# Top-k attention, dense layer and routed experts in one kernel: every batch in two groups of rows, epsilon on VectorE, loads and routing reordered

## The chip, the core and the metric

One core of a Trainium2 chip runs the whole program. TensorE (PE) multiplies, with its weight loads shown as a row of their own (PEld), VectorE (DVE) and ScalarE (ACT) do element work, GpSimd (POOL) does element work and issues some transfers, SyncE (SP) issues the others. The metric is the device time of one execution in microseconds (us).

## The reference

Three layers follow each other.

```python
scores = (q @ k.T) / 8                      # 4 batches, 8 heads, 576 rows, head size 64
mask = scores >= kth_largest(scores, 32)    # per row of 576
attn = exp(where(mask, scores, -1e9) - max)
x = attn / (attn.sum() + 1e-9) @ v          # -> 2304 tokens x 512
h = x @ w_in                                # 512 -> 2048
x = (max(h, 0) + alpha * min(h, 0)) @ w_out # 2048 -> 512
go = x @ w_skip > 0                         # which tokens take an expert
e = argmax(x @ w_gate)                      # which of 8 experts
out = x + go * gate[e] * relu(x @ w1[e]) @ w2[e]   # 512 -> 1024 -> 512
```

All products are computed in parts: each float32 operand is split into a high and a low part, and three matmuls (high by high, low by high, high by low) stand for one.

## The kernel before, in words

**Units.** The attention of one batch has four pairs of heads. A pair has five units: units 0 to 3 hold 128 rows of each of the two heads, unit 4 (the mixed one) the last 64 rows of both. `Unit` has one method per piece of work: `scores` (PE), `copy` (ACT), `fold` and four `round`s (DVE, they find the 32nd largest), `exp` (ACT), `weights` (DVE, mask and sum, L449), `eps` (ACT, L454, adds 1e-9 to the sum), `recip` (DVE, L458, and ACT's broadcast L461), `turn` (PE transposes), `evac` (ACT), `values` (PE), `out` (DVE, ACT, POOL).

**The order around it.** `main` walks over the units in steps. A step has 14 slots; the table `STEP` says in which slot which method runs, and for which unit relative to the step's own. Units are spread over about five steps: scores two steps ahead, values one step behind. In each slot `slot(q)` then issues pieces of the dense layer from the list `todo`, as many as the budget q allows. Over a step the budget is what is left divided by the steps that are left, at least BMIN = 4.3 and at most BMAX = 6.0 us by the kernel's own cost figures, and half of it in a step whose next unit is mixed. Six matmuls of n columns cost 6 n / 2400 us in this table. An engine does its instructions in the order in which they were issued.

**Groups.** `work` lists groups of rows: (batch, units, first column, column tiles). Batch 0 is two groups, units 0 and 1 (256 rows) and units 2 to 4 (320 rows). Batches 1 to 3 are one group each, with two column tiles of 288. For each group all four pairs are done, and each pair loads and turns q and k (`heads`: `load`, `turn` for q and k, `turn_t` for the last 64 rows). When a group's attention is complete, `queue_moe` puts its dense layer (`moe1`) on the list, so the dense layer of a batch is computed beside the attention of the next one; the dense layer of the last group has nothing left beside it.

**The dense layer.** `moe1` streams the weights in 16 chunks of 1 MB through three buffers (`wr`, issued by POOL, L525). A chunk serves all column tiles of the group: 48 matmuls of 288 columns for a group with two tiles, 24 matmuls for a group with one. With two tiles the hidden layer is done in two halves (`nhf = 2`), and the second half's result is added by POOL (L640); with one tile there is one pass.

**Rows and routing.** After a group's dense layer `rows` computes the routing scores (`logits`, PE), `route`, `rest` and `slots` (some 30 small DVE instructions) and writes the rows out. A hook, `pick`, runs after batch 2 and chooses the expert whose first block is prepared early.

**After the attention.** A loop calls `slot(TS)` until the lists are empty. It counts its turns (`gone`, from `pick` on): from the 39th turn it loads expert weights ahead (`wraw`, 0.5 MB each, issued by SP, L950), and splits them into high and low parts (ACT L956, DVE L957). Eleven blocks of 128 tokens follow: gather, first layer (L985), second layer (L1003), write.

**Buffers.** The input of the dense layer is a tile x per batch, two of them in turn. The first `out` of batch b waits until the dense layer of batch b - 2 is complete (`getx`), and issues what is left of it at once.

Of the kernel before, what the change touches and what calls it, by code (L numbers as in the profile page):

```python
# [35 lines left out]
AHEAD = 2  # L36
EC = 32
PH = 9
ECC = 1.9
CL = 2  # L40
# [9 lines left out]
HL = 3  # L50
# [9 lines left out]
def kernel(  # L60
# [240 lines left out]

    def heads(b, p, i):

        hd = dict(vb=vbd[i], qb=qbd[i])
        nats = {}

        def load():

            hd["q"] = att.tile([128, 2, SB], F32R, name="qT", tag="qT", bufs=2)
            hd["k"] = att.tile([128, 2, S + TL], F32R, name="kT", tag="kT", bufs=2)  # L310
# [16 lines left out]
        def turn(s):  # L327
            pt = ptile()
            for r in range(SF):
                nc.tensor.transpose(pt[:, r * 128:(r + 1) * 128], nats[s][:, r].rearrange("p h d -> p (h d)"), ident)  # L330
            c0 = TL
            late.append((HL, lambda: part(hd["k"][:, :, c0:c0 + SB] if s else hd["q"], pt)))

        def turn_t():
            pt = ptile()
            nc.tensor.transpose(pt[:, 0:128], nats[2].rearrange("p h d -> p (h d)"), ident)

            def copies():

                raw = att.tile([128, 512], F32, name="raw_", tag="raw_", bufs=2)[:, 0:TL]  # L340
# [5 lines left out]
                part(hd["k"][:, :, 0:TL], pt[:, TL:128])  # L346
                nc.gpsimd.tensor_copy(hd["k"][:, :, S:S + TL], hd["k"][:, :, 0:TL].bitcast(F32))

# [10 lines left out]
        hd["v"] = loadv  # L359
        return hd, [load, lambda: turn(0), lambda: turn(1), turn_t]  # L360

    class Unit:
# [317 lines left out]
    def rows(b, us, colof, x2t, hook, then):  # L680
# [394 lines left out]
    def main(work, exact, hooks=(lambda: [], lambda: [])):  # L1075

        if not exact:
# [4 lines left out]
            todo.insert(4, (0.5, late_consts))  # L1082
        steps, pairs, colofs, bases = [], [], [], []
        stream.clear()
# [4 lines left out]
        for wi, (b, us, col0, cols) in enumerate(work):  # L1089
# [5 lines left out]
            for p in range(NP):  # L1095
                pairs.append((b, p))
                for u in us:
                    steps.append((wi, len(pairs) - 1, u))
# [5 lines left out]
        hds, hq, vq = {}, [], {}  # L1104

        def push_heads(i):
            hd, parts = heads(*pairs[i], i % 2)
            hds[i] = hd
            hq.extend(parts)
            if i > 1:  # L1110

# [28 lines left out]
        def queue_moe(wi):  # L1140
# [11 lines left out]
            def then():  # L1152
                rowq.extend(rows(b, us, colofs[wi], x2t, hooks[1] if wi + 1 == len(work) else none[0],
                                 hooks[0] if wi + 2 == len(work) else none[0]))

# [29 lines left out]
        for kx in range(-2, K + 2):  # L1185
# [19 lines left out]
            for x in range(NSLOT):  # L1205
# [3 lines left out]
                for at, d, name, *a in STEP:  # L1209
                    if at != x:  # L1210
                        continue
                    if name == "heads":
                        for f in hmine:
                            f()
# [11 lines left out]

    T2 = [(0, 288), (288, 576)]
# [193 lines left out]
```

## Time and profile before

| | us |
|---|---|
| median of 3 runs | 1147.65 (1147.05 to 1148.07) |
| profiled execution, time | 1146.64 |
| its span, first to last instruction | 1144.8 |
| DVE busy in the span | 957.6 (84%) |
| PE busy | 976.2 (85%) |
| ACT busy | 738.7 (65%) |
| POOL busy | 453.9 (40%) |

The time is 1.84 us above the span. Shares over the whole span mix stages with different limits: attention (with the conversion of the dense layer's weights at its start), a stretch with the last dense layer alone, and the blocks of the experts. Busy time of PE is modelled and includes the depth of its pipeline. A line is a group of records of one source line; an idle time is put down to what ended it.

### The profile page before, as it was taken

Reading aid. Unit: us, or ns where it says so; the run is one execution under the profiler, and the core shown is the slowest. Engines: PE = TensorE matmul, PEld = TensorE weight load, DVE = VectorE, ACT = ScalarE, POOL = GpSimd, SP = SyncE. Lnnn points to the kernel's source line nnn. Section 1 sums busy time; section 2 is a strip of 40 time slices with the busy share of each in tenths; the row PEclk is TensorE's granted clock in tenths of the full one; section 3 lists DMA queues with packets and bytes.
Section 4 is the critical chain, followed back from the end, with each engine's and each line's share of the span. In section 5 each row is a group of like instructions: output and inputs, shape, how many; then the busy total and the mean of one; then the engine's idle time right before and its main releaser. Section 6 shows DMA issues by size and latency. Waiting matters only on the chain.

```text
span 1144.8 us, 21810 instructions
## 1 busy us (share of the span) xinstructions
PE 976.2 (85%) x7214; PEld 855.7 (75%) x7214; DVE 957.6 (84%) x2906; ACT 738.7 (65%) x1970; POOL 453.9 (40%) x591
## 2 busy tenths in 40 slices
PE   1255657989898987898998999899999999898996
PEld 1143436879777875787997998789899999687884
DVE  5799999999999999999999889999933331799872
ACT  5576666866777665776677567767734452597761
POOL 5445543643334331244235344423435343228111
PEclk9996566999999995899999999999999999799998
DMA  8977764567544530224324253332337863699870
GB/s 233 336 220 229 216 184 124 188 191 232 187 136 154 179 130 21 69 75 142 97 84 142 75 171 93 105 122 75 112 111 274 298 221 111 195 372 385 316 276 15
DMA packets 129771, 197.37 MB, mean 172 GB/s; under 512 B 62766, under 2 KB 92462, under 8 KB 119408
## 3 DMA queue, kind: packets, MB, share of 16 engines
q1 hardware_dynamic: 115632, 107.48, 29.9%
q0 software_dynamic: 14016, 88.40, 22.6%
q8 instruction: 59, 0.97, 0.3%
q14 instruction: 64, 0.52, 0.2%
HBM read 167.44 MB, written 29.71 MB: 172 GB/s over the span
## 4 chain that ended last, share of the span: by engine, by line
PE 42%; DVE 42%; ACT 5%; issue 4%; DMA 4%; POOL 2%; SPq 1%; POOLq 0%; DVEq 0%; ACTq 0%
PE pm L627 14%; DVE v L420 8%; PE pm L578 8%; DVE F L411 6%; DVE Ex L449 6%; DVE F L423 5%; DVE m L411 5%; PE px L1003 4%; PE pm L985 3%; PE px L510 3%; PE pt L476 3%; PE ps L390 3%; DVE rn L595 3%; DMA nat<-in_q_dram 2%; DVE cv L278 2%
## 5 line engine op out<-in xcount | busy, mean ns | idle before, releaser
L627 PE MATMUL pm<-g,wr 128*128 128x288 f32 (+2 forms) x1536 | 237.3, 303 | 7.2 <-POOL g L109 7.2
L578 PE MATMUL pm<-x,wr 128*128 128x288 f32 (+2 forms) x1536 | 238.9, 304 | 4.0 <-ACT x L519 2.9
L627 PEld LDWEIGHTS pm<-g,wr 128*128 128x128 f32 x1536 | 209.0, 189 | 15.1 <-POOL g L109 8.8
L578 PEld LDWEIGHTS pm<-x,wr 128*128 128x128 f32 x1536 | 211.2, 191 | 10.4 <-issue 5.3
L420 DVE MAX8 v<-F 128x8 f32<-128x72 f32 (+2 forms) x576 | 214.0, 406 | 1.0
L395 ACT ACTIVATE sb<-ps 128x288 f32<-128x288 f32 x288 | 104.9, 411 | 89.3 <-PE ps L390 70.3
L109 POOL TENSOR_TENSOR g<-rn,g 128x288 fp32r<-128x288 f32 (+2 forms) x128 | 108.2, 853 | 123.2 <-ACT g L609 52.5
L390 PE MATMUL ps<-kT,qT 64*128 64x288 f32 x768 | 106.4, 363 | 38.6 <-ACT sb L395 15.7
L449 DVE SCALAR_TENSOR_TENSOR Ex<-sb,v,Ex 128x576 f32<-128x576 f32 x144 | 124.5, 891 | 0.0
L423 DVE MATCH_REPLACE8 F<-v,F 128x72 f32<-128x72 f32 (+1 forms) x432 | 122.7, 289 | 0.0
L390 PEld LDWEIGHTS ps<-kT,qT 64*128 64x128 f32 x768 | 69.2, 210 | 68.2 <-ACT sb L395 19.8
L109 POOL TENSOR_TENSOR x<-xf,x 128x128 fp32r<-128x128 f32 (+1 forms) x80 | 38.7, 483 | 177.6 <-ACT x L519 164.6
L443 ACT ACTIVATE Ex<-sb,st 128x576 f32<-128x576 f32 x144 | 105.0, 780 | 0.0
L595 DVE SCALAR_TENSOR_TENSOR rn<-rn,nalpha 128x288 f32<-128x288 f32 (+2 forms) x128 | 72.5, 566 | 34.3 <-ACT rn L589 31.7
L476 PE MATMUL pt<-ident,Ex 128*128 128x128 f32 x576 | 92.6, 302 | 0.0
L510 PE MATMUL px<-PT,vt 128*64 128x128 f32 (+1 forms) x1280 | 92.0, 292 | 0.0
L488 ACT ACTIVATE PT<-pt 128x512 f32<-128x512 f32 x144 | 86.0, 598 | 2.3 <-PE pt L476 2.0
L588 ACT ACTIVATE rn<-pm 128x288 f32<-128x288 f32 (+2 forms) x128 | 52.7, 412 | 45.3 <-PE pm L578 44.6
L476 PEld LDWEIGHTS pt<-ident,Ex 128*128 128x128 f32 x576 | 72.2, 154 | 11.1 <-issue 6.5
L510 PEld LDWEIGHTS px<-PT,vt 128*64 128x64 f32 x1280 | 72.5, 150 | 10.2 <-issue 2.9
L411 DVE TENSOR_TENSOR F<-m 128x144 f32<-128x144 f32 (+2 forms) x240 | 78.2, 377 | 0.0
L609 ACT ACTIVATE g<-rn 128x288 fp32r<-128x288 f32 (+2 forms) x128 | 56.4, 448 | 23.0 <-DVE rn L595 22.9
(367 smaller groups left out, 1839.2 us busy)
## 6 DMA issues: line engine op xcount, KB each, us to landing
wraw<-in_moe_w_dram SPq DMA_DIRECT2D x88, 512.0 KB, 6.0
wr<-win POOLq DMA_DIRECT2D x40, 1024.0 KB, 5.2
wr<-wout POOLq DMA_DIRECT2D x40, 1024.0 KB, 5.2
cv<-in_moe_w_in_dram SPq DMA_DIRECT2D x16, 512.0 KB, 5.3
win<-cv SPq DMA_DIRECT2D x16, 512.0 KB, 5.4
cv<-in_moe_w_out_dram SPq DMA_DIRECT2D x16, 512.0 KB, 4.1
wout<-cv SPq DMA_DIRECT2D x32, 256.0 KB, 4.5
vt<-in_v_dram SPq DMA_DIRECT2D x20, 256.0 KB, 3.0
```

Source lines behind the costliest of these rows:

```text
L109: i = nc.gpsimd.tensor_tensor(o, a, b, op=OP.subtract)
L390: nc.tensor.matmul(self.ps[h, j][:, 0:HALF], lhsT=hd["q"][gp, a, u * 128:(u + 1) * 128], rhs=hd["k"][gp, b_, c0:c0 + HALF], **se)
L411: gate[0] = nc.vector.tensor_tensor(o[:, n_], a[:, n_, 0:w], a[:, n_, w:2 * w], op=op)
L420: nc.vector.max(v8[:, h, r, :], F[:, h, 0:w])
L423: nc.vector.match_replace(out=F[:, h, 0:w], in_to_replace=v8[:, h, r, :], in_values=F[:, h, 0:w], imm_value=NEG)
L443: nc.scalar.activation(self.Ex[:, h, :], self.sb[:, h, :], AF.Exp, bias=self.st[:, 0, h:h + 1], scale=0.125)
L449: nc.vector.scalar_tensor_tensor(Ex[:, h, :], sb[:, h, :], v8[:, h, 3, 7:8], Ex[:, h, :], op0=OP.is_ge, op1=OP.mult, accum_out=st[:, 1, h: ...
L476: nc.tensor.transpose(pt[:, c * 128:(c + 1) * 128], P[:, c0:c0 + 128], ident)
L510: nc.tensor.matmul(x[h * 64:(h + 1) * 64, 0:n], lhsT=hd["vt"][:, h, c, :], rhs=rhs, start=False, stop=(c == SF - 1))
L578: nc.tensor.matmul(hp[:, 0:n], lhsT=w[:, (f % 2) * 8 + a * 4 + d, :], rhs=x[:, d, c0:c1], start=(i == 0), stop=(i == 3 * KD - 1))
L595: nc.vector.scalar_tensor_tensor(rn[:, 0, 0:n], rn[:, 1, 0:n], nalpha[:, f:f + 1], rn[:, 0, 0:n], op0=OP.mult, op1=OP.add)
L627: nc.tensor.matmul(op_[:, 0:n], lhsT=w[:, 2 * f + a, :], rhs=g[(hf + ch) * 8 + f, sg][:, gg, 0:n], start=(i == 0), stop=(i == ni - 1))
```

## The change

- `work` gives every batch as two groups, units 0 and 1 (one tile of 256 columns) and units 2 to 4 (one tile of 320). There are eight groups and 32 pairs for five groups and 20 pairs.
- `heads` loads and turns only the q rows of its own group; k is loaded and turned whole for each group, and q's last 64 rows only where unit 4 is in it. The loads of a pair are put on SP's list one pair earlier, and the turns are split over two slots of a step.
- `eps` (ACT) goes; `recip` does the addition on DVE, and moves from slot 5 to slot 2, ahead of round 0. ACT's broadcast stays in slot 5 as `spread`.
- `route` follows `logits` three slots later, for one (RD).
- `pick` is tied to the last group of batch 2.

```diff
+RD = 3
+WHOLE = ()
-        (1, 2, "copy", 0), (1, -1, "eps"),
-        (2, 1, "round", 0),
+        (1, 2, "copy", 0),
+        (2, -1, "recip"), (2, 1, "round", 0),
...
-        (5, -1, "recip"), (5, -1, "turn", 1),
+        (5, -1, "spread"), (5, -1, "turn", 1),
...
-        (10, 0, "heads"), (10, 0, "weights", 0), (10, -1, "evac", 2),
+        (10, 0, "heads", 0), (10, 0, "weights", 0), (10, -1, "evac", 2),
         (11, 0, "weights", 1),
+        (12, 0, "heads", 1),
...
-    def heads(b, p, i):
+    def heads(b, p, i, us):
...
+        full = [u for u in us if u < SF]
+        own = ((full[0], full[-1] + 1), (0, SF))
...
+                r0, r1 = own[s]
                 for h in range(2):
-                    nc.sync.dma_start(nat[:, :, h, :], src[b, 2 * p + h, 0:SB, :].rearrange("(p r) d -> p r d", p=128))
+                    nc.sync.dma_start(nat[:, r0:r1, h, :],
+                                      src[b, 2 * p + h, 0:SB, :].rearrange("(p r) d -> p r d", p=128)[:, r0:r1])
...
-        def eps(self):
-            st = self.st
-            nc.scalar.activation(st[:, 1, self.n_], st[:, 1, self.n_], AF.Copy, bias=1e-9)
-
         def recip(self):
             st = self.st
+            nc.vector.tensor_scalar(st[:, 1, self.n_], st[:, 1, self.n_], 1e-9, None, op0=OP.add)
             nc.vector.reciprocal(st[:, 2, self.n_], st[:, 1, self.n_])
+
+        def spread(self):
+            st = self.st
...
-        parts = [(lambda: not early[0] and rroom(), None), (0.1, logits), (0, None), (0.1, route)]
+        parts = [(lambda: not early[0] and rroom(), None), (0.1, logits)] + [(0, None)] * RD + [(0.1, route)]
...
-    work = [(0, [0, 1], 0, [(0, 256)]), (0, [2, 3, 4], 256, [(256, 576)])]
-    for b in range(1, B - 1):
-        work.append((b, [0, 1, 2, 3, 4], 0, T2))
-    work.append((B - 1, [0, 1, 2, 3, 4], 0, T2))
+    work = []
+    for b in range(B):
+        if b in WHOLE:
+            work.append((b, [0, 1, 2, 3, 4], 0, [(0, 288), (288, 576)]))
+        else:
+            work += [(b, [0, 1], 0, [(0, 256)]), (b, [2, 3, 4], 256, [(256, 576)])]
```

Three places show what moves. On DVE, in a step of the attention, before (L458 is the reciprocal, 420 and 423 the rounds, 517 the multiplication of `out`):

```order
L411 TENSOR_TENSOR F<-m 128x2x72 x2
L420 MAX v_4423<-F 128x8 x2
L423 MATCH_REPLACE F<-v_4423,F 128x72 x2
L420 MAX v_4423<-F 128x8 x2
L423 MATCH_REPLACE F<-v_4423,F 128x72 x2
L458 RECIPROCAL st<-st 128x1
L517 TENSOR_TENSOR xf<-px,R 128x128
```

And the same place now (L467 adds the epsilon, L468 is the reciprocal, L433 and L436 are the rounds):

```order
L424 TENSOR_TENSOR F<-m 128x2x72 x2
L467 TENSOR_SCALAR st<-st 128x2
L468 RECIPROCAL st<-st 128x2
L433 MAX v_4771<-F 128x8 x2
L436 MATCH_REPLACE F<-v_4771,F 128x72 x2
L433 MAX v_4771<-F 128x8 x2
L436 MATCH_REPLACE F<-v_4771,F 128x72 x2
L530 TENSOR_TENSOR xf<-px,R 128x128
```

The reciprocal now stands two rounds earlier and has the addition ahead of it. On PE, the end of the attention before (L476 to L482 are turns, L506 and L510 values, L627 the dense layer's second product, here of batch 2):

```order
L627 MATMUL pm<-g,wr 128x288 x12
L506 MATMUL px<-PT,vbd_93 128x128
L510 MATMUL px<-PT,vt 64x128 x8
L627 MATMUL pm<-g,wr 128x288 x18
L476 MATMUL pt<-ident,Ex 128x128 x4
L627 MATMUL pm<-g,wr 128x288 x18
L481 MATMUL pt<-ident,Ex 64x128
L482 MATMUL pt<-ident,st 128x128
L627 MATMUL pm<-g,wr 128x288 x18
L506 MATMUL px<-PT,vbd_93 128x64
L510 MATMUL px<-PT,vt 64x64 x8
L627 MATMUL pm<-g,wr 128x288 x18
```

And now (L640 is the second product, here of the first group of batch 3):

```order
L640 MATMUL pm<-g,wr 128x256 x18
L519 MATMUL px<-PT,vbd_93 128x128
L523 MATMUL px<-PT,vt 64x128 x8
L640 MATMUL pm<-g,wr 128x256 x18
L489 MATMUL pt<-ident,Ex 128x128 x4
L640 MATMUL pm<-g,wr 128x256 x24
L494 MATMUL pt<-ident,Ex 64x128
L495 MATMUL pt<-ident,st 128x128
L640 MATMUL pm<-g,wr 128x256 x12
L519 MATMUL px<-PT,vbd_93 128x64
L523 MATMUL px<-PT,vt 64x64 x8
L640 MATMUL pm<-g,wr 128x256 x12
```

The dense layer that runs out here is of a group of the same batch, in as many matmuls. What PE has to do behind it, before (L578 is the first product, L693 the routing scores, L712 rows):

```order
L712 MATMUL ps<-ident,x2t 64x128 x4
L578 MATMUL pm<-x,wr 128x288 x180
L627 MATMUL pm<-g,wr 128x288 x192
L578 MATMUL pm<-x,wr 128x288 x192
L627 MATMUL pm<-g,wr 128x288 x192
L693 MATMUL ps<-wg,x2t 128x9 x16
L693 MATMUL ps<-wg,x2t 64x9 x4
```

And now (L591 is the first product, L706 the routing scores, L725 rows, L785 and L786 ranks, L1269 a flag):

```order
L706 MATMUL ps<-wg,x2t 128x9 x8
L591 MATMUL pm<-x,wr 128x320 x12
L725 MATMUL ps<-ident,x2t 128x128 x8
L785 MATMUL ps<-oh,tri 128x16
L786 MATMUL ps<-oh,ones 128x16
L591 MATMUL pm<-x,wr 128x320 x6
L1269 MATMUL pt<-ones,fl 1x1
L591 MATMUL pm<-x,wr 128x320 x174
L640 MATMUL pm<-g,wr 128x320 x192
L706 MATMUL ps<-wg,x2t 128x9 x8
L706 MATMUL ps<-wg,x2t 64x9 x4
```

768 matmuls of 288 columns have become 384 of 320; the other 384 (of 256 columns) stand in the attention.

## Rows read from the trace of the kernel before

**Rows 1.** Windows by stage: batches 0 to 3, dense layer alone, blocks.
```profile
core 0: us, PE busy (x) PEld busy (x) DVE busy (x) ACT busy (x) POOL busy (x), PEclk, DMA share, GB/s
0.00:278.70 278.70, 173.52 (x1172) 139.89 (x1173) 251.59 (x705) 185.25 (x502) 132.59 (x164) 0.83 0.71 214
278.70:461.40 182.70, 161.15 (x1292) 138.60 (x1290) 180.06 (x665) 122.24 (x367) 61.59 (x95) 0.93 0.43 137
461.40:651.10 189.70, 175.12 (x1478) 157.54 (x1477) 183.92 (x625) 134.12 (x410) 74.75 (x102) 0.97 0.31 97
651.10:839.40 188.30, 182.01 (x1561) 165.55 (x1560) 179.03 (x631) 132.11 (x402) 74.67 (x111) 0.99 0.35 114
839.40:986.10 146.70, 142.17 (x1070) 138.43 (x1068) 42.51 (x153) 61.84 (x157) 59.48 (x85) 0.96 0.60 207
986.10:1144.80 158.70, 142.23 (x652) 115.71 (x652) 120.47 (x132) 103.12 (x132) 50.79 (x35) 0.94 0.73 266
```

**Rows 2.** Windows: the same for L449 alone, one batch (36 instructions, two records each).
```profile
651.10:839.40 188.30, 29.43 (x72) 0.99 0.35 114
```

**Rows 3.** Windows: five units with no dense layer beside them.
```profile
430.20:471.40 41.20, 31.61 (x199) 24.01 (x199) 41.03 (x149) 25.43 (x76) 8.85 (x13) 0.67 0.08 20
```

**Rows 4.** Waits of DVE up to 839 us: total us, times, longest.
```profile
DVE st L458 <- ACT st L454: 13.9, 11, 2.8
DVE rc L737 <- ACT lg L702: 3.9, 1, 3.9
DVE rc L737 <- ACT lg L700: 1.2, 1, 1.2
```

**Rows 5.** Windows: the first `out` of batch 3 (columns as in rows 1).
```profile
625.00:650.00 25.00, 22.12 (x179) 20.17 (x178) 22.02 (x82) 11.96 (x37) 8.81 (x12) 0.93 0.25 85
650.00:675.00 25.00, 25.00 (x222) 23.20 (x222) 18.93 (x64) 13.34 (x41) 9.78 (x13) 1.00 0.39 124
```

**Rows 6.** DVE's groups: busy us, mean ns of one, idle before.
```profile
L595 DVE SCALAR_TENSOR_TENSOR rn<-rn,nalpha 128x256 f32<-128x256 f32 x16 | 8.6, 538 | 0.4 <-ACT rn L589 0.4
L458 DVE RECIPROCAL st<-st 128x2 f32<-128x2 f32 x64 | 9.9, 154 | 9.5 <-ACT st L454 9.5
```

**Rows 7.** Timeline of DVE: first and last instruction of one routing of five units.
```profile
976.31 0.20 DVE L737 TENSOR_REDUCE rc<-lg 128x5 f32<-128x40 f32 x1 [20.61 <-ACT lg L702]
...
980.55 0.16 DVE L790 TENSOR_TENSOR cnt<-tot,e_row 128x8 f32<-128x8 f32 x1
```

**Rows 8.** Longest, shortest of L449 (ns min/median/max), and one group each of DVE, POOL.
```profile
L449 DVE SCALAR_TENSOR_TENSOR Ex<-sb,v,Ex x144: 791/808/2335, 56.4 to 838.5; 128x576 f32<-128x576 f32 x144
...
L449 DVE SCALAR_TENSOR_TENSOR Ex<-sb,v,Ex 128x576 f32<-128x576 f32 x144 | 124.5, 891 | 0.0
...
L109 POOL TENSOR_TENSOR kT<-raw__8684,kT 128x512 fp32r<-128x512 f32 x1 | 1.4, 1435 | 0.0
```

**Rows 9.** The chain in order of time: start us, us, what (x matmuls).
```profile
836.79 0.22 PE px L506 x2
837.01 1.02 PE px L510 x16
...
840.61 0.44 PE pt L476 x4
...
855.66 2.57 PE pm L627 x18
...
894.70 25.50 PE pm L627 x192
...
971.95 4.05 PE ps L693 x40
```

**Rows 10.** Timeline of PE: six score matmuls.
```profile
542.37 0.66 PE L390 MATMUL ps<-kT,qT 64*128 64x288 f32 x6
```

**Rows 11.** Weight chunks: KB, median us to landing; a window with expert weights loading.
```profile
wr<-wout POOLq DMA_DIRECT2D x40, 1024.0 KB, 5.2
...
875.00:897.00 22.00, 21.23 (x160) 20.99 (x160) 6.97 (x13) 14.25 (x41) 15.97 (x21) 1.00 0.99 352
```

More of the change, by code (lines that the diff above doesn't have):

```diff
@@ L299, in convert @@
         return none * (CV - 1) + [bits] + none * (CV - 1) + [split] + none * (2 * CV) + [store]
-    def heads(b, p, i):
+    def heads(b, p, i, us):
         hd = dict(vb=vbd[i], qb=qbd[i])
+        full = [u for u in us if u < SF]
+        own = ((full[0], full[-1] + 1), (0, SF))
         nats = {}
         def load():
-            hd["q"] = att.tile([128, 2, SB], F32R, name="qT", tag="qT", bufs=2)
-            hd["k"] = att.tile([128, 2, S + TL], F32R, name="kT", tag="kT", bufs=2)
             tail = att.tile([128, 2, D], F32, name="nat_t", tag="nat_t", bufs=2)
@@ L327, in turn @@
         def turn(s):
[L328 to L332, printed above, removed]
+            if s == 0:
+                hd["q"] = att.tile([128, 2, SB], F32R, name="qT", tag="qT", bufs=2)
+                hd["k"] = att.tile([128, 2, S + TL], F32R, name="kT", tag="kT", bufs=2)
+            r0, r1 = own[s]
+            c0, c1 = r0 * 128, r1 * 128
+            pt = ptile()[:, c0:c1]
+            for r in range(r0, r1):
+                nc.tensor.transpose(pt[:, r * 128 - c0:(r + 1) * 128 - c0], nats[s][:, r].rearrange("p h d -> p (h d)"),
+                                    ident)
+            late.append((HL, lambda: part(hd["k"][:, :, TL:TL + SB] if s else hd["q"][:, :, c0:c1], pt)))
         def turn_t():
@@ L338, in copies @@
             def copies():
+                part(hd["k"][:, :, 0:TL], pt[:, TL:128])
+                nc.gpsimd.tensor_copy(hd["k"][:, :, S:S + TL], hd["k"][:, :, 0:TL].bitcast(F32))
+                if SF not in us:
+                    return
                 raw = att.tile([128, 512], F32, name="raw_", tag="raw_", bufs=2)[:, 0:TL]
@@ L345, in copies @@
                     sub(hd["qb"][gp, 1, gp], raw[gp], hd["qb"][gp, 0, gp].bitcast(F32))
-                part(hd["k"][:, :, 0:TL], pt[:, TL:128])
-                nc.gpsimd.tensor_copy(hd["k"][:, :, S:S + TL], hd["k"][:, :, 0:TL].bitcast(F32))
             late.append((HL, copies))
@@ L359, in heads @@
         hd["v"] = loadv
-        return hd, [load, lambda: turn(0), lambda: turn(1), turn_t]
+        hd["load"] = load
+        return hd, [lambda: turn(0), lambda: turn(1), turn_t]
     class Unit:
@@ L1082, in main @@
             todo.insert(4, (0.5, late_consts))
-        steps, pairs, colofs, bases = [], [], [], []
+        steps, pairs, pairs_of, colofs, bases = [], [], [], [], []
         stream.clear()
@@ L1096, in main @@
                 pairs.append((b, p))
+                pairs_of.append(wi)
                 for u in us:
@@ L1104, in main @@
         hds, hq, vq = {}, [], {}
+        ahead = {}
         def push_heads(i):
-            hd, parts = heads(*pairs[i], i % 2)
+            if not ahead:
+                ahead[i] = heads(*pairs[i], i % 2, work[pairs_of[i]][1])
+                hq.append(ahead[i][0]["load"])
+            hd, parts = ahead.pop(i)
             hds[i] = hd
             hq.extend(parts)
+            if i + 1 < len(pairs):
+                ahead[i + 1] = heads(*pairs[i + 1], (i + 1) % 2, work[pairs_of[i + 1]][1])
+                hq.append(ahead[i + 1][0]["load"])
             if i > 1:
@@ L1153, in then @@
                 rowq.extend(rows(b, us, colofs[wi], x2t, hooks[1] if wi + 1 == len(work) else none[0],
-                                 hooks[0] if wi + 2 == len(work) else none[0]))
+                                 hooks[0] if b == B - 2 and us[-1] == SF else none[0]))
             parts = moe1(xs_[b], cols, x2t, bases[wi]) + [(0, None), (0.0, done), (0.0, then)]
@@ L1212, in main @@
                     if name == "heads":
-                        for f in hmine:
+                        for f in hmine[a[0]::2]:
                             f()
@@ L1225, in main @@
         release()
-    T2 = [(0, 288), (288, 576)]
-    work = [(0, [0, 1], 0, [(0, 256)]), (0, [2, 3, 4], 256, [(256, 576)])]
-    for b in range(1, B - 1):
-        work.append((b, [0, 1, 2, 3, 4], 0, T2))
-    work.append((B - 1, [0, 1, 2, 3, 4], 0, T2))
+    work = []
[4 more added lines that the diff above has]
+            work += [(b, [0, 1], 0, [(0, 256)]), (b, [2, 3, 4], 256, [(256, 576)])]
     def swap():
```

## The prediction

> **What bounds the kernel now.** I read the busy times by stage first, then the waits of DVE, then the chain of work in order of time, then single groups and stretches of the timeline for prices. The profiled execution took 1146.64 us, 1.84 us more than its span; the median of the runs shown is 1147.65, so a sum made against the profile stands 0.1% under it.
>
> By stage the reader sees three kernels in one [rows 1]. In the attention of batches 1 to 3 DVE is busy 180.06 of 182.70, 183.92 of 189.70 and 179.03 of 188.30 us: DVE is the bound, with PE close behind (161, 175 and 182 us). From 839.4, where the last mask is done, to 986.1 DVE is busy 42.5 of 146.7 us and PE 142.2: here PE does the last dense layer alone. The blocks take the last 158.7 us. A batch has 36 mask instructions [rows 2], which is how I set the borders.
>
> So the change gives PE's work of the second stage to the first, where DVE sets the pace, and the question is what the first stage pays for it.
>
> **Prices.** Five units without a dense layer beside them take 41.2 us with DVE busy 41.0 [rows 3]; the mixed unit has half the columns, so a full unit costs DVE 41.2 / 4.5 = 9.2 us. On PE, 192 dense matmuls of 288 columns take 25.50 us [rows 9], 0.133 us each; in proportion to the columns 0.148 for 320 and 0.118 for 256, so a batch costs the same. A full unit's attention costs PE twice 0.66 for the scores [rows 10], twice 0.44 and 0.22 for the turns, 0.22 and 1.02 for the values [rows 9]: 3.7 us.
>
> **The first stage.** DVE's added work:
> - The epsilon, 80 instructions. The nearest row is the reciprocal of the same two columns, 154 ns [rows 6]: 12.3 us. The reciprocal has to wait for it, so it does not overlap; bounds 0.13 us (routing's pace, below) and 0.2 us each, 11 to 16.
> - The hidden layer of batch 3's first group comes in: 16 instructions of 538 ns [rows 6], 8.6 us.
> - Routing. A group of n units takes 22 + 2n instructions, and 32 of them run from 976.31 to 980.71 [rows 7], 0.138 us each. Before, three groups were routed in this stage (86 instructions), now six (162): 76 x 0.138 = 10.5 us.
>
> Together 31.4 us. DVE's removed waits: for ACT's epsilon 13.9 us in 11 times, and for the routing scores 3.9 and 1.2 [rows 4], the latter since `route` comes three slots later. At batch 3's first `out` PE runs on with what is left of batch 1's dense layer and DVE is idle 3.0 + 6.1 us [rows 5]; now batch 1's second group is done beside batch 2's first one and this goes, 8.5 us after taking off the half microsecond that any such window loses. Sum 27.5. These waits end on ACT and PE, and nothing else stands right behind them, so I count them whole; if ACT is late again at the rounds' end, half of the first would return.
>
> Two things are added that no row shows directly. The first is balance. The dense layer is no longer even over a batch: beside the eight steps of units 0 and 1 stand the 320 columns of the group before. At the budget's cap of 6.0 a step takes 45 matmuls: 45 x 0.148 + 3.7 + 0.5 for turns of q and k = 10.8 us of PE. While these are of the first product DVE needs 9.2 + 4 x 0.6 = 11.6 (0.54 is the row for 256 columns [rows 6]) and hides it; in the 3.4 steps of the second product it needs 9.2, and waits 1.6: 5.4 us a group, 16 for three. In the last two steps of units 2 to 4 the table gives 54 to 60 matmuls of 256 columns, 20 us of PE against 13.8 of DVE: 6.3, or 19 for three. If nothing evens out that is 35 us. Scores are made two units ahead, so part of it does: bounds 0 and 35. The nearest row is batch 3 of before, where PE was busy 97% and DVE still 95% of the time; I take 20.
>
> The second is POOL. Twelve more turns of k bring 12 x 1.435 = 17 us of subtractions [rows 8], their small parts and the issues of 48 more weight chunks up to twice as much again: 17 to 52 us. Mask instructions take 808 ns at the median and 891 in the mean, and up to 2335 [rows 8]: 144 x 83 ns = 12 us of stretch beside the 344 us that POOL is busy up to 839 [rows 1]. If the folds show as much, 7% of POOL's time comes back as DVE's, 1 to 4 us of the added; I take 4. The Trainium skill (SBUF — State Buffer, "Who interferes with whom") says that an instruction of DVE with two inputs in SBUF and one of GpSimd that reads SBUF lock each other out for the whole instruction. The trace agrees that there are long ones, and shows 83 ns of it in the mean; by the rule taken at its worst the whole of the added time would count, which is a rival below.
>
> ACT loses 80 epsilons and gains the turns of k; it is busy 132 of 189 us in batch 2 [rows 1], and I cost it at nothing. The added turns on PE are in its 0.5 us a step. The loads of q and k are a pair earlier on SP's list and have a pair's time (18 us or more) to land: nothing; without that cover a pair would wait a landing, 5 us at most by the weights' row [rows 11].
>
> First stage: 31.4 - 27.5 + 20 + 4 = +27.9 us, bounds -9 (no imbalance, no stretch, old waits gone, cheap epsilons) and +61 (35 of imbalance, half of the epsilon waits back, dear epsilons, 17 of POOL's).
>
> **The second stage.** Before, from 839.4:
> - 18.8 us to 858.2, the end of the attention on PE with 102 matmuls of batch 2 [rows 9]. Now it is 102 of 256 columns: 1.5 less, 17.3.
> - 113.7 us to 971.95, 768 matmuls (102.0) and 11.7 of rows and routing. Now 384 x 0.148 = 56.7, and 7.5 for the rows of two units: scores 4.05 us for 4.5 units' worth [rows 9] become 1.8, rows and ranks go down likewise.
> - 14.2 us to the first block, now 11.9 for 2.5 units' worth.
>
> That is 93.4 for 146.7. What no row shows is whether the weights come in time. A 1 MB chunk served 48 matmuls, 6.4 us; now 24 of 320 columns, 3.5 us, or 296 GB/s, while the expert weights are loaded ahead in the same stretch, where 352 GB/s and a DMA share of 0.99 are seen [rows 11]. 14 chunks and 14 expert loads are 22 MB, 62.6 us at that rate, against 64.2 of PE: at best nothing is lost. If the two streams share evenly for the 41 us that 7.3 MB of experts then take, seven chunks take 6.0 us instead of 3.5: 17 us. I take the middle, 8. The Trainium skill (DMA: Bandwidth & Descriptors, "Queues, rings and completion order") says that each DMA engine takes turns between queues packet by packet, which would put the loss towards the 17; no run here shows the share yet.
>
> Second stage: 101.4, so -45.3 us (bounds -53 and -36). **Blocks:** two of 16 expert loads are issued later than before, 1 MB at 352 GB/s: +3 (0 to 8). The rest is unchanged.
>
> **Sum:** 1146.64 + 27.9 - 45.3 + 3 = 1132 us. With half of the way to either bound of balance (10 and 7.5) and of the weights (4 and 4.5) its own range is 1118 to 1144. What a measurement of this kernel can tell from no change is about 0.2%, 2.3 us.
>
> **Rivals.**
> - *Evened out.* PE's surplus is spread by the two units' lead, the weights come in time, the blocks start with all loads: 1132 - 20 - 8 - 3 = 1101. For it: PE at 97% beside DVE at 95% in batch 3. Against: DVE idle 6.1 us as soon as PE has a whole stretch at 25.00 of 25 [rows 5].
> - *Starved tail.* Weights are shared evenly (17 for 8) and the blocks start late (8 for 3): 1146, no change. For it: a DMA share of 0.99 already [rows 11]. Against: PE still busy 21.2 of 22 us there.
> - *Unbalanced steps.* All 35 us are paid: 1147, no change.
> - *POOL holds DVE* (slower). Each added POOL instruction stops DVE for its length, 34 us, the middle of 17 to 52, for 4: 1162. It decides from 18 us of added stretch on, about half of the added POOL time. For it: mask instructions of 2335 ns. Against: a mean only 83 ns over the median.
>
> **How the numbers follow.** Forecast 0.45, evened out 0.17, starved tail 0.11, unbalanced 0.11, POOL 0.16. Faster: the first two and a little of the two at the border, less the upper end of the forecast's range, 0.66; same 0.11; slower 0.23. The range goes from the evened-out case to near POOL's, 1101 to 1159.
>
> **What would show it.** The last mask at about 867 us (864 to 870 supports the first stage's sum; 847 the evened-out case; over 885 POOL or imbalance, told apart by the mask's mean, over 950 ns for POOL, and by DVE's idle time in the second-product steps for imbalance). No waits of DVE for ACT's epsilon, none of 6 us at a first `out`. From the last mask to the first block about 101 us, with 57 us for 384 matmuls if weights are in time and up to 74 if not, and then PE waiting for `wr`. The prediction is wrong if the first stage grows by more than the second shrinks, or if the second still takes over 125 us.

## The result, and the profile after

The changed kernel takes 1135.82 us in the median of four runs (1132.73 to 1137.22), the kernel before 1147.86 beside it (four runs, 1147.05 to 1151.54): a ratio of 0.9894, 95% interval 0.9866 to 0.9921. The forecast was 1132, with a range from 1101 to 1159. Run again on another chip the ratio was 0.9905 (0.9868 to 0.9941). The profiled execution took 1132.73 us, 1.9 more than its span.

The windows by stage of the changed kernel answer to [rows 1]; the borders are again the last masks of the batches, and the first block's first correction of its input on DVE.

```profile
core 0: us, PE busy (x) PEld busy (x) DVE busy (x) ACT busy (x) POOL busy (x), PEclk, DMA share, GB/s
0.00:267.20 267.20, 166.63 (x1170) 134.74 (x1170) 244.43 (x724) 181.22 (x475) 122.95 (x157) 0.86 0.72 221
267.20:466.60 199.40, 190.92 (x1607) 171.92 (x1607) 193.16 (x703) 139.64 (x421) 96.10 (x144) 0.98 0.63 200
466.60:670.70 204.10, 195.18 (x1654) 176.00 (x1654) 190.98 (x701) 141.04 (x424) 97.49 (x146) 0.99 0.64 207
670.70:867.30 196.60, 186.70 (x1578) 168.29 (x1577) 185.47 (x688) 133.08 (x397) 92.37 (x138) 0.99 0.62 203
867.30:968.00 100.70, 88.01 (x619) 83.42 (x617) 31.96 (x116) 37.81 (x88) 33.58 (x49) 0.95 0.85 302
968.00:1130.80 162.80, 142.16 (x652) 115.66 (x652) 120.57 (x132) 102.98 (x132) 51.21 (x34) 0.93 0.71 262
```

The last mask comes at 867.3 us for 839.4, the stage behind it takes 100.7 for 146.7, the blocks 162.8 for 158.7: +27.9, -46.0 and +4.1, close to what was forecast (+27.9, -45.3, +3). But the first number is made of two that were not: batch 0 became 11.5 us shorter (267.2 for 278.7), and batches 1 to 3 became 39.4 us longer (600.1 for 560.7). In those DVE is busy 569.6 us for 543.0 and idle 30.5 for 17.7, and PE is busy 572.8 us for 518.3. PE now has as much to do there as DVE.

The second stage shrank because the work left at the last mask did. These two windows count the matmuls of the dense layer's second product in that stage, before and after (PE busy, instructions):

```profile
core 0: us, PE busy (x), PEclk, DMA share, GB/s
839.40:986.10 146.70, 68.02 (x496) 0.96 0.60 207
```

```profile
core 0: us, PE busy (x), PEclk, DMA share, GB/s
867.30:968.00 100.70, 43.81 (x297) 0.95 0.85 302
```

With the first product, 384 before (52.09 us) and 192 after (31.30), it is 880 matmuls before and 489 after.

DVE's waits up to the last mask, after (total us, times, longest), answer to [rows 4]:

```profile
DVE cv L281 <- ACT cv L277: 13.6, 4, 5.6
DVE rc L750 <- ACT lg L715: 9.0, 3, 3.4
...
DVE rc L750 <- ACT lg L713: 5.3, 2, 2.7
DVE xf L530 <- PE px L523: 4.8, 5, 1.3
```

The 13.9 us for ACT's epsilon are gone. The waits for the routing scores `lg`, 5.1 us before, are 14.3 us now.

The epsilon on DVE, one group for each shape (busy us, mean ns):

```profile
L467 DVE TENSOR_SCALAR st<-st 128x2 f32<-128x2 f32 x64 | 18.8, 294 | 0.0
L467 DVE TENSOR_SCALAR st<-st 128x1 f32<-128x1 f32 x16 | 2.3, 144 | 0.0
```

That is 21.1 us, where 12.3 had been forecast; the median of all 80 is 158 ns, the longest 1284. The timelines of DVE and of POOL at one of the long ones show why:

```profile
327.88 1.25 DVE L467 TENSOR_SCALAR st<-st 128x2 f32<-128x2 f32 x1
329.17 0.17 DVE L468 RECIPROCAL st<-st 128x2 f32<-128x2 f32 x1
```

```profile
327.65 1.47 POOL L112 TENSOR_TENSOR kT<-raw__4015,kT 128x512 fp32r<-128x512 f32 x1 [2.50 <-DVE F L424]
```

POOL's subtraction starts 0.24 us before the epsilon and ends at 329.12, and the epsilon ends at 329.13. Ten of the 80 take over 400 ns. Each of the ten starts 0.08 to 0.24 us behind the start of a POOL subtraction and ends within 0.03 us of its end. They sum to 9.6 us, which is 8.0 us over ten times the median. So the epsilon costs about 13 us of its own and 8 us of standing behind POOL.

### The profile page after: what moved, and what is told of

Same layout as the page of the kernel before. It is cut to its first block, busy times and chain, and to the rows that moved or that the text cites. A ratio compares the mean times of both kernels' runs of the same rounds, so it can differ in the third digit from the quotient of the medians.

```text
span 1130.8 us, 22345 instructions
## 1 busy us (share of the span) xinstructions
PE 969.6 (86%) x7270; PEld 850.0 (75%) x7270; DVE 966.6 (85%) x3055; ACT 735.8 (65%) x1932; POOL 493.7 (44%) x667
## 4 chain that ended last, share of the span: by engine, by line
PE 46%; DVE 31%; DMA 8%; ACT 6%; issue 4%; POOL 2%; SPq 1%; POOLq 0%; DVEq 0%; ACTq 0%
PE pm L640 13%; PE pm L591 10%; DVE v L433 6%; DVE Ex L462 4%; PE px L523 4%; PE ps L403 4%; PE px L1016 4%; DVE F L436 4%; DVE F L424 4%; PE pm L998 4%; PE pt L489 3%; DMA wr<-wout 3%; DVE m L424 3%; DVE rn L608 2%; DVE cv L282 2%
## 5 line engine op out<-in xcount | busy, mean ns | idle before, releaser
L591 PE MATMUL pm<-x,wr 128*128 128x256 f32 (+1 forms) x1536 | 248.2, 308 | 12.3 <-DMA wr<-win 4.7
L640 PE MATMUL pm<-g,wr 128*128 128x256 f32 (+1 forms) x1536 | 240.7, 304 | 3.6 <-DMA wr<-wout 2.9
L591 PEld LDWEIGHTS pm<-x,wr 128*128 128x128 f32 x1536 | 214.0, 192 | 22.1 <-issue 5.3
L640 PEld LDWEIGHTS pm<-g,wr 128*128 128x128 f32 x1536 | 209.8, 189 | 13.0 <-issue 7.1
L433 DVE MAX8 v<-F 128x8 f32<-128x72 f32 (+2 forms) x576 | 214.2, 409 | 1.0
L403 PE MATMUL ps<-kT,qT 64*128 64x288 f32 x768 | 103.5, 358 | 52.0 <-ACT sb L408 35.0
L112 POOL TENSOR_TENSOR g<-rn,g 128x256 fp32r<-128x256 f32 (+1 forms) x128 | 109.6, 867 | 74.7 <-ACT g L622 28.6
L436 DVE MATCH_REPLACE8 F<-v,F 128x72 f32<-128x72 f32 (+1 forms) x432 | 123.5, 293 | 0.0
L608 DVE SCALAR_TENSOR_TENSOR rn<-rn,nalpha 128x256 f32<-128x256 f32 (+1 forms) x128 | 74.4, 582 | 25.3 <-ACT rn L602 25.3
L523 PE MATMUL px<-PT,vt 128*64 128x128 f32 (+1 forms) x1280 | 88.5, 285 | 0.0
L601 ACT ACTIVATE rn<-pm 128x256 f32<-128x256 f32 (+1 forms) x128 | 52.7, 412 | 48.7 <-PE pm L591 44.6
L489 PEld LDWEIGHTS pt<-ident,Ex 128*128 128x128 f32 x576 | 69.5, 149 | 10.9 <-issue 6.2
L622 ACT ACTIVATE g<-rn 128x256 fp32r<-128x256 f32 (+1 forms) x128 | 56.4, 449 | 26.1 <-DVE rn L608 25.8
L424 DVE TENSOR_TENSOR F<-m 128x144 f32<-128x144 f32 (+2 forms) x240 | 68.8, 339 | 0.0
```

The source lines that it names most:

```text
L112: i = nc.gpsimd.tensor_tensor(o, a, b, op=OP.subtract)
L403: nc.tensor.matmul(self.ps[h, j][:, 0:HALF], lhsT=hd["q"][gp, a, u * 128:(u + 1) * 128], rhs=hd["k"][gp, b_, c0:c0 + HALF], **se)
L424: gate[0] = nc.vector.tensor_tensor(o[:, n_], a[:, n_, 0:w], a[:, n_, w:2 * w], op=op)
L433: nc.vector.max(v8[:, h, r, :], F[:, h, 0:w])
L436: nc.vector.match_replace(out=F[:, h, 0:w], in_to_replace=v8[:, h, r, :], in_values=F[:, h, 0:w], imm_value=NEG)
L489: nc.tensor.transpose(pt[:, c * 128:(c + 1) * 128], P[:, c0:c0 + 128], ident)
```

## The experiments

Ratios are to the kernel before on the same chip. e1 to e4 shared a chip, so did e5, e7, e8 and e9, and so did e10, e11 and the second runs of the changed kernel and of e2.

**e1: an even budget.** The planner's budget is pinned at 5.2 from batch 1 on, in place of 4.3 to 6.0.

```diff
-q = min(max(q, BMIN), BMAX) * (...) / NSLOT
+lo, hi = (5.2, 5.2) if steps[min(max(kx, 0), K - 1)][0] > 1 else (BMIN, BMAX)
+q = min(max(q, lo), hi) * (...) / NSLOT
```

> The changed kernel with the dense layer's budget fixed at 5.2 us a full step from batch 1 on (4.3 to 6.0 before), so that each batch's two groups are spread evenly over its units. Theory (balance: the forecast's 20 us for steps in which PE is the bound): batches 1 to 3 take about 585 us instead of 600, the time falls from 1136 to about 1122. Rival (DVE's added instructions and routing make the whole growth): 598 to 602 us, time 1133 to 1139. Second rival (the budget was what kept the groups from overtaking each other, and what is left over goes to the end): last mask earlier, but the stretch to the first block longer by the same, time unchanged.

Measured: 1142.40 us (1140.96 to 1147.56), ratio 0.9923 (0.9896 to 0.9950). The last mask comes at 870.2, and batches 1 to 3 take 602.5 us for 600.1. But the edit evens little: counted between masks and priced by the kernel's own figures, a step of units 0 and 1 holds 5.0 us of dense matmuls in the mean where the changed kernel has 5.4, a step of units 2 and 3 has 4.0 for 3.8. This small shift buys nothing; an even plan was not run.

**e2: without the epsilon.** The 1e-9 is not added anywhere.

```diff
-nc.vector.tensor_scalar(st[:, 1, self.n_], st[:, 1, self.n_], 1e-9, None, op0=OP.add)
```

> The changed kernel without the addition of 1e-9 (the 80 small DVE instructions are left out; nothing takes their place). In the trace of the changed kernel they last 294 ns for two columns (64 times) and 144 ns for one (16 times), 21 us in all, where the forecast had 12.3. If DVE is the bound throughout: time 1136 - 21 = 1115. If DVE is the bound only part of the time and 12 of 21 are on the path: 1124. If PE is the bound since the dense layer was moved: 1133 to 1137.

Measured: 1129.82 us (1124.79 to 1133.12), ratio 0.9802 (0.9775 to 0.9830). In its profile the last mask comes at 865.9, only 1.4 us earlier, so the ratio and the stages did not agree; it was run again, beside the changed kernel on one chip:

> The changed kernel itself once more, as the measure for the three kernels beside it on the same chip. Ratio 0.987 to 0.992, as before.

> The kernel without the 1e-9 (it is not added anywhere), now on the same chip as the changed kernel. Theory 1: the epsilon's 21 us of VectorE lie on the path, and the earlier ratio of 0.980 stands: 8 to 12 us below the changed kernel. Theory 2: in batches 1 to 3 PE and the steps that route set the pace (without the epsilon the last mask came at 865.9 for 867.2, 1.4 us earlier), so the difference is 0 to 4 us.

Measured: the changed kernel 1137.83 us (1134.64 to 1145.62), ratio 0.9905; without the epsilon 1130.45 (1127.03 to 1133.84), ratio 0.9836 (0.9809 to 0.9864). The difference, 7.4 us, lies between the two theories. The second profiles, of the changed kernel and then without the epsilon, give batches 1 to 3 and the stage behind them:

```profile
266.90:872.10 605.20, 576.65 (x4831) 520.03 (x4827) 571.24 (x2087) 413.23 (x1237) 287.27 (x428) 0.98 0.63 201
872.10:983.40 111.30, 92.12 (x620) 87.91 (x618) 32.22 (x119) 37.77 (x88) 33.60 (x49) 0.91 0.79 273
```

```profile
264.30:860.00 595.70, 572.20 (x4835) 516.57 (x4834) 558.36 (x2027) 413.74 (x1238) 288.52 (x428) 0.99 0.64 205
860.00:962.40 102.40, 88.61 (x622) 84.18 (x620) 32.04 (x118) 37.82 (x88) 33.61 (x49) 0.94 0.85 297
```

Over the two pairs of profiles the last mask is 1.4 and 12.1 us earlier without the epsilon, 6.8 in the mean, which the medians bear out. By the two ratios of the first runs, on different chips (0.9802 and 0.9894), it would be 10.6 us. So a third to a half of the epsilon's 21 us is on the path. The same kernel's last mask moved by 4.8 us from one profile to the next (867.3, 872.1) and its second stage by 10.6 (100.7, 111.3): a stage of one profile is no measure for less.

**e3: the epsilon on ACT again,** with the reciprocal in slot 5, the rest of the change as it is.

```diff
-        (1, 2, "copy", 0),
-        (2, -1, "recip"), (2, 1, "round", 0),
+        (1, 2, "copy", 0), (1, -1, "eps"),
+        (2, 1, "round", 0),
...
-        (5, -1, "spread"), (5, -1, "turn", 1),
+        (5, -1, "recip"), (5, -1, "spread"), (5, -1, "turn", 1),
```

> The changed kernel with the epsilon back on ACT in slot 1 and the reciprocal back in slot 5, all else as changed. By the forecast the two prices nearly cancel (12.3 us of DVE for 13.9 of waits): 1133 to 1139. By the measured length of the additions (21 us) the old form is the better one: about 1129. Rival (the earlier reciprocal frees ACT and with it PE, and this is what made batch 0 11.5 us shorter): batch 0 back from 267 to about 277 us, time 1145 or more.

Measured: 1139.55 us (1134.21 to 1143.92), ratio 0.9889 (0.9859 to 0.9919), no different from the changed kernel. DVE waits for it 20.3 us in 16 times up to the last mask. Moving the epsilon to DVE traded 20 us of waits for 21 us of work. Batch 0 ends at 269.4 us, not at the 277 of the rival.

**e4: no early expert weights.** They are loaded only when the dense layer is done.

```diff
-TL0 = 38
+TL0 = 100000
...
+    loads()
     until(1, 0)
```

> The changed kernel without loading expert weights ahead in the stretch of the last dense layer; the first eight loads are issued after it. Theory (the two streams share the DMA engines): from the last mask to the first block's start 101 us fall to about 88, the waits of PE for weight chunks go, the 384 dense matmuls take 57 to 60 us instead of 72; the blocks start without weights and take 25 to 35 us more, time 1147 to 1158. Rival (chunks come late because of POOL's order or the three buffers, not of the experts' loads): the dense matmuls still take 68 us or more.

Measured: 1144.19 us (1141.54 to 1147.21), ratio 0.9921 (0.9891 to 0.9951). PE's waits from the last mask to the first block, in the changed kernel, in its second profile, and here:

```profile
PE pm L591 <- DMA wr<-win: 4.7, 3, 2.3
...
PE pm L640 <- DMA wr<-wout: 1.8, 3, 0.9
```

```profile
PE pm L640 <- DMA wr<-wout: 6.6, 3, 4.0
PE pm L591 <- DMA wr<-win: 6.4, 2, 3.8
```

```profile
PE pm L998 <- ACT xs L989: 21.2, 1, 21.2
...
PE pm L591 <- DMA wr<-win: 1.2, 2, 0.7
...
PE pm L640 <- DMA wr<-wout: 0.4, 2, 0.2
```

Without the early loads the chunks `wr` come nearly in time (1.6 us of waits for 6.5 and 13.0), so the two streams do compete. From the routing scores of batch 3's first group to those of its second PE takes 66.1 us here, 72.6 in the changed kernel and 82.9 in its second profile, so the matmuls came down less than the theory had it (57 to 60 for 72). What this saves is lost at the first block, which now waits 21.2 us. The time stays under the 1147 to 1158 of the theory, and the ratio is not told apart from the changed kernel's.

**e5: everything but the groups.** Batches 1 to 3 are whole again.

```diff
-WHOLE = ()
+WHOLE = (1, 2, 3)
```

> The changed kernel with batches 1 to 3 as one group each again (batch 0 is two groups in both kernels), so that the step table, VectorE's epsilon, the loads and parts of a pair and the routing parts act alone. By the working of the prediction the edits other than the groups take 27.5 us of waits away and add 12 to 21 us of epsilon; the last mask comes 6 to 15 us before the 839 us of the kernel before, the second stage stays at about 147 us plus 159 us of blocks: ratio 0.987 to 0.995. Rival: the groups carry the whole gain, and the other edits are worth nothing or cost what the epsilon adds: ratio 1.00 to 1.01. In both the first batch should end near 267 us, as in the changed kernel, if its gain of 11.5 us came from these edits and not from what follows it.

Measured: 1145.84 us (1140.68 to 1149.72, ten runs), ratio 0.9976 (0.9953 to 0.9999). By stage:

```profile
0.00:267.30 267.30, 168.69 (x1187) 136.22 (x1187) 245.68 (x724) 182.46 (x477) 123.54 (x158) 0.87 0.71 221
267.30:835.40 568.10, 526.97 (x4299) 467.68 (x4296) 551.78 (x1979) 381.80 (x1114) 207.80 (x306) 0.94 0.36 114
835.40:987.10 151.70, 143.43 (x1066) 139.23 (x1064) 45.29 (x156) 61.80 (x156) 59.93 (x85) 0.95 0.58 200
```

Batch 0 ends at 267.3, as in the changed kernel, so its gain is of the other edits. Those are worth 0.24% together, between the two expectations; in batches 1 to 3 they even cost 7.4 us (568.1 for 560.7, one profile each). The groups take 32.0 us more in batches 1 to 3 (600.1 for 568.1) and give 51.0 back behind the last mask; against the second profile of the changed kernel it is 37.1 and 40.4. By the ratios (0.9976 against 0.9894 and 0.9905) the groups are worth 8 to 9 us. They carry the larger part of the result.

**e9: groups in batches 0 and 3 alone.**

```diff
-WHOLE = ()
+WHOLE = (1, 2)
```

> Only batches 0 and 3 are two groups, batches 1 and 2 are whole. Theory: each grouped batch costs the first stage about 13 us (batches 1 to 3 grew by 39.4 us), and only the last batch's groups shorten the second stage, so this keeps the second stage near 264 us and its first stage ends 16 to 26 us earlier than 867 us: about 1108 to 1118 us in the changed kernel's own run, ratio 0.967 to 0.977. Rival: the dense work of batch 2, routed only at its end, now lands in batch 3's steps beside that of its first group, so what the first stage gains comes back in the second: ratio 0.987 to 0.995.

Measured: 1187.55 us (1186.51 to 1189.91), ratio 1.0341 (1.0304 to 1.0378). Both expectations missed it by far. The rival had the place right and the size wrong. From the last mask on:

```profile
857.90:1028.50 170.60, 138.13 (x979) 132.90 (x978) 48.88 (x178) 57.82 (x147) 59.76 (x88) 0.90 0.74 264
1028.50:1184.50 156.00, 139.07 (x652) 113.54 (x652) 120.48 (x132) 102.02 (x131) 51.22 (x34) 0.96 0.74 271
```

```profile
PE pm L591 <- DMA wr<-win: 20.4, 5, 9.1
PE pm L640 <- DMA wr<-wout: 4.3, 5, 1.8
```

785 dense matmuls (384 and 401) are left at the last mask, nearly the 880 of before, although batch 3 has its two groups. Batch 2's dense layer, routed only at that batch's end, uses up batch 3's steps, and both groups of batch 3 are left whole, with 17 matmuls of batch 2. PE then waits 24.7 us for chunks, and batch 3 itself takes 210.9 us (647.0 to 857.9) for 189.2 in e5 (646.2 to 835.4). Here the split of the last batch does not pay while the batch before it is whole.

**e8: the epsilon in another form,** `tensor_tensor` with a constant tile.

```diff
-nc.vector.tensor_scalar(st[:, 1, self.n_], st[:, 1, self.n_], 1e-9, None, op0=OP.add)
+nc.vector.tensor_tensor(st[:, 1, self.n_], st[:, 1, self.n_], epsc[:, self.n_], op=OP.add)
```

> The epsilon is added on VectorE from a constant tile of 1e-9 (tensor_tensor of 128x2) in place of tensor_scalar with an immediate. Theory 1: the 294 ns of the 128x2 tensor_scalar (144 ns for 128x1) come from the form of the instruction; tensor_tensor of 128x2 takes 140 to 170 ns, which frees about 9 us of VectorE and 5 to 9 us of the time: ratio 0.981 to 0.986. Theory 2: they come from waiting for the sums that the masks before it have just written; then it stays near 290 ns and the ratio at 0.989.

Measured: 1139.85 us (1136.08 to 1141.54), ratio 0.9925 (0.9896 to 0.9954). One line of the profile decides (ns min/median/max):

```profile
L469 DVE TENSOR_TENSOR st<-st,epsc x80: 142/149/1270, 67.3 to 871.3; 128x2 f32<-128x2 f32 x64, 128x1 f32<-128x1 f32 x16
```

Both theories were wrong. The instruction is short in the median in this form (149 ns) as in the other (158), and 14 of 80 take over 400 ns, each from just behind the start of a POOL subtraction to its end. Nine of the 14 have two columns, five have one. In the changed kernel five one-column additions stand behind the same subtractions and are not held; DVE and POOL at one of them, in the changed kernel and then here:

```profile
445.07 0.14 DVE L467 TENSOR_SCALAR st<-st 128x1 f32<-128x1 f32 x1
444.90 0.84 POOL L112 TENSOR_TENSOR g<-rn,g 128x256 fp32r<-128x256 f32 x1 [1.95 <-DVE F L424]
```

```profile
446.18 0.73 DVE L469 TENSOR_TENSOR st<-st,epsc 128x1 f32<-128x1 f32 x1
446.01 0.87 POOL L112 TENSOR_TENSOR g<-rn,g 128x256 fp32r<-128x256 f32 x1 [1.43 <-DVE F L426]
```

So for one column the form decides: all five take 139 to 155 ns with `tensor_scalar` and 683 to 729 with `tensor_tensor`, to within 0.03 us of the subtraction's end.

**e7: the routing earlier** (`RD = 1`) **and e10: later** (`RD = 8`).

```diff
-RD = 3
+RD = 1        # e7; e10: RD = 8
```

> One empty part in place of three between the logits and the routing of a group. Theory: the routing waits on VectorE for the logits longer (the waits for lg of 9.0 and 5.3 us in all grow by 1 to 3 us for each of 8 groups, 8 to 16 us): ratio 0.996 to 1.003. Rival: those waits are hidden by the steps' other work, or the earlier routing gives the dense steps their work earlier: ratio 0.986 to 0.992, as the changed kernel.

> Eight empty parts in place of three between a group's logits and its routing. Theory: VectorE's waits for lg (14.3 us in five waits up to the last mask) go, the last mask comes 8 to 14 us earlier than 867 us, ratio 0.977 to 0.983. Rival: the routing then runs where VectorE is full and the dense steps behind it start later, so what is saved at lg is paid elsewhere: last mask at 862 to 872 us, ratio 0.987 to 0.993.

Measured: e7 1138.59 us, ratio 0.9903 (0.9868 to 0.9938), e10 1139.44, ratio 0.9918 (0.9892 to 0.9943); neither differs from the changed kernel. In e7 the waits for `lg` are 26.3 us in six times, 12.0 more than in the changed kernel, as its theory had it, and yet the time is not longer. In e10 the waits for `lg` are gone, and DVE's other waits up to the last mask have grown in their place:

```profile
DVE rn L608 <- ACT rn L602: 9.9, 6, 3.0
...
DVE tot L797 <- PE pm L786: 5.6, 3, 3.5
DVE rc L767 <- ACT rt L756: 5.4, 4, 2.0
DVE xf L530 <- PE px L523: 5.4, 4, 2.3
```

These sum to 26.3 us; in the changed kernel the same four and `lg` are 22.7. The last mask came at 870.4. The rival was right.

**e11: all of q for each group.** A group loads, turns and splits all four rows of q.

```diff
-own = ((full[0], full[-1] + 1), (0, SF))
+own = ((0, SF), (0, SF))
```

> Each group loads, turns and splits all four rows of q again, not only its own. Theory: batch 0 got its 11.5 us from POOL: the split of q was twice 512 columns a pair and is now 256 for the first group, POOL's busy time from the first step's end to the first group's end fell by 9.5 us and VectorE's adds, shifts and masks there by as much. Then batch 0 ends at 274 to 280 us in this kernel, and the groups of batches 1 to 3 lose up to as much each (last mask 880 to 910 us, ratio 1.00 to 1.03). Rival: the gain of batch 0 came from the new step table and the split of heads over two slots; batch 0 stays at 266 to 269 us and the ratio at 0.988 to 0.994.

Measured: 1147.67 us (1142.68 to 1151.65, ten runs), ratio 0.9987 (0.9971 to 1.0004), 9.8 us over the changed kernel beside it. The last mask comes at 877.6, and batch 0 ends at 270.5. The eight profiles of kernels with the same batch 0 as the changed kernel's end it between 266.7 and 269.2, so 1 to 4 us of its 11.5 are q, not the 7 to 13 of the theory and not the nothing of the rival. POOL's subtraction for q is 128x512 there, 1.5 us in the mean (1.27 to 1.86), where the changed kernel has 128x256, 1.0 us (0.73 to 1.31). Whether it costs its time on POOL, on PE (which turns two more rows) or through DVE was not told apart. Parts of a pair are what lets the groups pay: without them the whole change is worth 0.13%, not told apart from nothing.

## Why the prediction was right, and where it was not

**The time and the direction** came out, and the mechanism is the one described: PE's work of the second stage moves into the first, for less than it cost alone.

**The second stage** held in each part in the first profile. The routing scores of batch 3's two groups mark the parts on PE:

```profile
883.79 1.92 PE L706 MATMUL ps<-wg,x2t 128*128 128x9 f32 x16
...
956.35 2.53 PE L706 MATMUL ps<-wg,x2t 128*128 128x9 f32 x24
```

From the last mask to the end of the attention it takes 16.5 us (17.3 forecast), to the second scores 72.6 (56.7, 7.5 and 8, together 72.2), to the first block 11.7 (11.9). In all 101.4 us were forecast and 100.7 and 111.3 measured, the second of these just beyond the bound of -36 (110.7). Of waits for chunks 8 us were forecast (bounds 0 and 17), and 6.5 and 13.0 measured. The other 4.1 us between the two profiles are PE's busy time (88.01 and 92.12), with a granted clock of 0.95 and 0.91. The chain after shows four chunks on it:

```profile
894.27 9.54 DMA wr<-win
909.91 7.34 DMA wr<-win
930.55 6.61 DMA wr<-wout
945.59 7.09 DMA wr<-wout
```

Turns packet by packet, as the Trainium skill has them (DMA: Bandwidth & Descriptors, "Queues, rings and completion order"), would have been the 17; both profiles stay under it. e4 shows that it is the early loads that the chunks compete with. The blocks' +3 was 4.1 in the one profile and 1.1 in the other.

**The first stage** is where steps failed, in both directions.

*The epsilon* (12.3 us, bounds 11 to 16) was mis-sized: 21.1 us. The 13 us of the instructions themselves were right. Missing were the 8 us behind POOL, since the nearest row, the reciprocal with its 154 ns, is not held by POOL (162 to 169 ns over all 80 in the profile after, though 18 of them start inside a POOL subtraction), and the epsilon is. The Trainium skill (SBUF — State Buffer, "Who interferes with whom") says that a DVE instruction with two inputs in SBUF and a GpSimd instruction that reads SBUF exclude each other for a whole instruction, and so do a `tensor_scalar` in a mode that uses both ports and a GpSimd instruction, while a DVE instruction with a single input in SBUF outside such modes does not contend. The trace agrees in what it can show: two-column epsilons in either form were held to the end of POOL's subtraction, the 128x1 ones with `tensor_scalar` were not (144 ns in the mean), and with `tensor_tensor` they were (e8). Which mode an instruction ran in no trace shows. The prediction had weighed the rule only for the masks.

*The removed waits* (27.5 us). The 13.9 for ACT's epsilon went. The 8.5 us at batch 3's first `out` were counted twice. These are all of DVE's waits in the kernel before from 625 to 676 us, around the windows of [rows 5]:

```profile
DVE st L458 <- ACT st L454: 5.3, 2, 2.8
DVE rc L737 <- ACT lg L702: 3.9, 1, 3.9
```

DVE's idle 3.0 and 6.1 us there are two waits for ACT's epsilon (2.81 and 2.51) and the wait for `lg`, of which 3.56 us lie before 675. All of them stand in [rows 4] and in the 13.9 and 3.9 already. Counted once, 19.0 us were to go, and the sum would have been about 1141. (The same 6.1 us are named against the evened-out rival; no `out` waits in them.) The 5.1 for `lg` were to go, since the routing comes three slots later, and became 14.3. For one thing, six groups now route in batches 1 to 3 where three did, and five of the six wait (2.7 to 3.4 us each). For another, a group's scores are now made in steps where PE has no room: 14 us of such a step show PE busy 13.47 and DVE 9.33.

```profile
479.00:493.00 14.00, 13.47 (x126) 11.75 (x124) 9.33 (x51) 9.68 (x27) 4.20 (x6) 1.00 0.63 218
```

e7 and e10 add that the routing may come earlier or later: 26.3, 14.3 or no us of waits for `lg` go with the same time. Start-up and the conversion of the weights apart (`ident`, `nalpha`, `cv`), DVE's waits up to the last mask did not fall by 27.5 us but rose from 19.4 to 24.0.

*Balance* (20 us, bounds 0 and 35) failed in its second part. The last two steps of units 2 to 4 were to hold 54 to 60 dense matmuls each and to keep DVE waiting 6.3 us. They hold 64 together (the table halves the budget of a step whose next unit is mixed, and unit 3's step holds 16), 8.99 us of PE, and DVE is busy 14.36 of their 14.60 us:

```profile
656.10:670.70 14.60, 14.11 (x127) 12.82 (x127) 14.36 (x57) 9.47 (x30) 5.25 (x8) 1.00 0.67 214
```

So the rival of unbalanced steps was wrong; the evened-out one gets no support from e1, which evened only a little. By the lengths of the steps, what takes the place of this term is the steps that route: six in batches 1 to 3, of 13.3 to 17.1 us, where the kernel before has three (13.5, 14.6 and 16.3) and the steps that do not route take 6 to 13 (but for the last, 1.4). The other is PE as the second bound: taking 17 us of epsilons out of batches 1 to 3 made them 1.8 us longer in one pair of profiles and 9.5 shorter in the other.

*POOL* (4 us). It became busy 75 us longer in batches 1 to 3 (286.0 for 211.0), above the 17 to 52 that were counted, and the rival that each added us stops DVE fell all the same. The mask, with its mean and extremes as in [rows 8], did not grow (in batches 1 to 3, where POOL's time was added, it fell from 91.9 to 87.2 us in all, and in batch 0 it rose from 33.3 to 37.2):

```profile
L462 DVE SCALAR_TENSOR_TENSOR Ex<-sb,v,Ex x144: 795/812/1820, 59.2 to 866.4; 128x576 f32<-128x576 f32 x144
...
L462 DVE SCALAR_TENSOR_TENSOR Ex<-sb,v,Ex 128x576 f32<-128x576 f32 x144 | 123.7, 887 | 0.0
```

In batches 1 to 3 the hidden layer (56.8 us for 47.1, forecast +8.6) and the epsilon (17.6) make up DVE's +26.6 already, so what routing added must be balanced elsewhere; the mask's 4.7 us are a part. Of what POOL's added time costs, the epsilon's 8 us are the part that the traces show.

*Batch 0* was not in the sum as a gain at all; the terms give it about -1.5 (20 epsilons against 4.6 us of waits). Most of the 11.5 lies in seven steps of its first group: 107.6 us before (57.9 to 165.5), 96.7 after (62.2 to 158.9), while the step ahead of them grew by 4.3. DVE never waits in these, before or after; POOL is busy 53.41 and 43.87 us in them, and DVE's integer operations on the weights' bits (L279 and L278, now L282 and L281) take 1175 and 1007 ns in the mean before, 979 and 749 after, in 37 instructions and 35. The masks there go the other way, from 1052 to 1356 ns. In the eight profiles with the same batch 0 these steps take 96.7 to 97.7 us, so small differences can be read. The rows of q that are no longer split here are a small part: with them (e11) it is 98.3 us. With the epsilon on ACT and the reciprocal back in slot 5 (e3) it is 100.0, so their move gives about 3 of the 10.9 us. That the new order of the steps makes DVE and POOL meet less often would fit; no run undid the rest of the order (the turns in two slots, the loads a pair earlier), so the larger part stays open.

So the first stage's +27.9 was right as a sum and wrong in its parts: batch 0 11.5 us better, and batches 1 to 3 39.4 longer. Added up by place, the terms give DVE 32.3 us more work in batches 1 to 3 (9.2 for epsilons, 8.6, 10.5 and 4), 2.9 us less idle time there (20 of balance less 22.9 of waits) and -1.5 in batch 0. Measured were +26.6, +12.8 and -11.5. The errors, -5.7, +15.7 and -10.0, cancel: that the sum came out to a tenth of a microsecond is luck. Its bounds are no sums of the terms named beside them either, which give +2.6 and +66.6 for -9 and +61.

## What to carry to other kernels

When work is moved from a stage with one busy engine into a stage that another engine bounds, count what is left over at the border: 880 matmuls against 489 is the gain here, and in e9 785 were left, with 24.7 us of waits for their chunks. Look at what ends an idle stretch before adding it to a list of waits: it may stand there already. Price a small instruction by what runs beside it on POOL as well as by its nearest neighbour in shape. A sum that comes out is no proof of its terms: two parts of the first stage with opposite errors looked like one right one.

## What was not expected of the hardware

A DVE addition of two columns, 0.16 us in the median, took up to 1.28 us when it started just behind a POOL subtraction: 10 of 64 took over 0.4 us in the changed kernel, and 9 of 64 in the form with two input tiles (e8). Of one column, none of 16 did as `tensor_scalar`, and 5 of 16 with two input tiles. The reciprocal right behind them, the same size, never did (162 to 169 ns over all 80).
